# Two-chunk k/v loads, small vectors loaded contiguous and transposed, swaps partly by engine copies, the first layer norm on GpSimd as multiply-add, another planned order

## The chip, the cores and the metric

The kernel runs on one core of a Trainium2 chip. The metric is the device time of one execution in microseconds (us). Most executions of one kernel agree within 1%; a run is marked slow when it lies over 1.5% above the fastest run of the same kernel, and verdicts use the other ("fast") runs.

A core has engines that each execute their own instruction list strictly in order: TensorE (PE; its weight loads are shown as PEld), VectorE (DVE), ScalarE (ACT), GpSimd (POOL) and SyncE (SP, which here only issues DMAs). An instruction waits for semaphores that other engines or DMAs raise.

## The reference

S = 2048 positions, D = 640 channels, F = 1728, all bf16. Cut to what matters:

```python
def mix(q, k, v, shift_k, ssm_k, ssm_D):          # q is already normalized
    k_shift = sum(shift_k[:, 3 - t] * k_pad[:, t:t + S, :] for t in range(4))   # 4-tap causal filter
    kv = k_shift * v
    y = irfft(rfft(kv, 2 * S) * rfft(ssm_k, 2 * S))[:S]     # long convolution per channel
    return q * (y + kv * ssm_D)

h  = x + mix(layernorm(x), k, v, shift_k, ssm_k, ssm_D)     # x is A_q
hn = layernorm(h)
r  = hn @ w_r;  idx = top-2 positions of r                  # 2 of the 2048 positions
y  = (silu(hn[idx] @ w_gate) * (hn[idx] @ w_up)) @ w_down * sigmoid(r[idx])
out = h + hn, with y added at the two positions idx
```

## The kernel before

The 640 channels are worked on in five chunks of 128 ("chunk 0" to "chunk 4"). The convolution of a chunk is a Fourier transform written as matmuls:

1. **S1**: first stage, once for the filter and once for kv.
2. **S2**: second stage, with the constant matrix F. F is loaded compact (F2c) and expanded into four masked copies at the start ("F expansion").
3. The two **swaps** of the chunk: the spectrum of the filter lies with real parts in partitions 0 to 63 and imaginary parts in 64 to 127; a copy with the halves exchanged goes to KfB. Then the products **P1** (A times A) and **P2** (A times KfB).
4. **I1**, **I2**: the inverse, as matmuls; then I2m (times the normalized q) and I2a (the residual add).
5. A transpose and the "gram" matmuls that yield sums for the second layer norm. After the last chunk follows a serial tail: norm statistics, top-2, the small feed-forward and the output.

Every operation is declared with the engines that may run it. A list of numbers, PLAN, holds one number for each operation: bits for its place in a single global order, for its engine and for its PSUM region. Semaphore waits are derived from it. So PLAN decides the order on every engine, and each engine obeys it literally.

```python
# F expansion: 16 tiles of 1024, any of ScalarE, VectorE, GpSimd
for kq in range(4):
    for lp in range(4):
        ...
        flex(lambda e, ...: e.activation(o, i, ACTF.Copy, scale=m),
             lambda e, ...: e.tensor_scalar(o, i, m, None, op0=ALU.mult), ..., name="F2x", pool=True)

# the swap: two DMAs, in SyncE's list
for h in range(2):
    dma("sp", KfB[64*h:64*h+64, c % 2], A2[64-64*h:128-64*h, ks], ...,
        writes=[buf("KfB", c % 2, h)] + [buf("P2", c % 2, b) for b in range(2)], name="sw%d" % c)

# the products: P2 on VectorE whole, or on GpSimd in four pieces of 128x512
op("dve", lambda e: e.tensor_tensor(dst[:, :, blk], A[:, :, blk], dst[:, :, blk], ALU.mult), ...)   # P1
em["pool"] = [part(g, g + 8) for g in range(0, NG, 8)]                                             # P2

# first layer norm ("LN1"), 16 tiles; nb = -mean*rd exists already, for ScalarE's form
flex(lambda e, n2=n2: e.activation(q_sb[:, n2, :], x_sb[:, n2, :], ACTF.Identity, bias=nb[...], scale=rd[...]),
     lambda e, n2=n2: e.tensor_scalar(q_sb[:, n2, :], x_sb[:, n2, :], m32[...], rd[...],
                                      op0=ALU.subtract, op1=ALU.mult), ..., name="q", pool=True)
```

Both swap DMAs of a chunk declare that they write the same P2 buffers, so the second one waits until the first has landed.

Of the kernel before, what the change touches and what calls it, by code (L numbers as in the profile page):

```python
# [17 lines left out]
    1376, 3536, 1504, 1680, 4048, 1728, 3920, 3472, 608, 8, 1816, 2000, 408, 3344, 3408, 456, 6872, 352, 6096, 3856, 648, 2704, 2632, 160, 2760, 6145,  # L18
    6224, 2896, 2312, 7234, 6936, 7304, 7000, 7064, 2184, 96, 7107, 2952, 3032, 2264, 2520, 736, 2392, 544, 6592, 2456, 6721, 784, 6664, 7184, 3984,
    7554, 7427, 6792, 1312, 3088, 3280, 6336, 6408, 928, 976, 288, 7632, 2584, 6465, 6536, 224, 7504, 8130, 1040, 3216, 8200, 11608, 3152, 7392, 8000,  # L20
    8072, 1632, 11843, 11672, 2840, 2072, 16472, 7745, 7816, 11920, 1440, 3664, 3792, 7874, 7944, 8512, 8584, 3600, 848, 3728, 8643, 8897, 8968, 4112,
    6304, 10832, 9154, 4304, 4240, 16536, 16600, 16664, 2136, 11736, 1880, 4176, 8768, 8840, 1120, 10881, 9232, 8712, 10960, 9024, 9096, 8258, 8387,
    8456, 8336, 12000, 12064, 11800, 12320, 11329, 11400, 4624, 11456, 11528, 12128, 4368, 4432, 4496, 4560, 4688, 4744, 12192, 12256, 12419, 12496,
    12546, 1944, 12384, 11073, 11144, 21336, 11200, 12624, 11272, 4816, 4880, 5400, 5592, 5336, 16707, 21400, 16784, 12866, 12936, 21464, 21528,
    12737, 12816, 11040, 15696, 12995, 9312, 13120, 13200, 7712, 5953, 6032, 15746, 15824, 13064, 14019, 14088, 13632, 13704, 13249, 13328, 13890,
    13960, 14147, 14216, 16192, 9376, 9552, 9624, 5080, 13505, 13584, 17120, 13378, 13448, 16928, 5208, 5712, 13763, 9424, 9488, 13832, 16264, 5912,
    15937, 5528, 16066, 16136, 17056, 17184, 16008, 16864, 16992, 17283, 17360, 17408, 26072, 17488, 1184, 9794, 17248, 16323, 16400, 9921, 9864,
    14304, 5016, 26136, 17600, 17986, 17859, 9992, 21569, 17680, 18056, 5840, 17928, 15904, 17728, 17800, 1248, 10050, 14368, 21648, 21792, 9667,
    9736, 10128, 21920, 18497, 18240, 18312, 18754, 5272, 20560, 18627, 18696, 18576, 5784, 19009, 19080, 18368, 18440, 21728, 18883, 18832, 14544,
    14480, 18114, 18184, 20609, 20688, 10176, 18952, 10434, 10504, 20801, 14616, 5464, 20931, 20872, 21000, 5656, 10256, 21984, 14416, 21856, 22048,  # L30
    22144, 21186, 21256, 12704, 22224, 5144, 22273, 22352, 14787, 14856, 14912, 14984, 4952, 10320, 10384, 22658, 22728, 21057, 21136, 22787, 22856,
    19168, 22112, 26304, 26384, 22530, 22600, 19232, 22401, 22480, 10576, 20768, 25360, 14659, 14728, 15040, 10640, 15112, 23682, 22913, 22992, 23752,
    23299, 23368, 26464, 25408, 25488, 23042, 23112, 23553, 23632, 23811, 23880, 19280, 23424, 23496, 15170, 15248, 23169, 23240, 25667, 25736, 15360,
    25921, 25794, 25864, 15440, 25539, 26656, 26200, 25992, 19344, 26264, 19480, 26592, 26528, 26784, 26720, 26816, 17568, 26896, 26946, 27024, 19416,
    19521, 25608, 19592, 19648, 19720, 23968, 24032, 15504, 27459, 27536, 27330, 27400, 27201, 27072, 27280, 30176, 30240, 27144, 19907, 19976, 19778,
    28097, 28168, 24144, 19856, 28352, 28424, 24280, 28483, 28560, 27585, 27656, 27970, 28048, 27712, 27784, 27843, 27920, 28225, 1568, 28296, 28640,
    15312, 10690, 24080, 24208, 10760, 20032, 20112, 20227, 15553, 20304, 20368, 20176, 28704, 28752, 28944, 28880, 28816, 15624, 30658, 24576, 24449,
    24648, 24520, 24323, 24704, 20417, 24776, 24392, 30720, 20488, 25024, 25104, 24835, 24912, 29377, 29448, 24976, 25168, 28992, 29064, 29249, 29123,
    29328, 25216, 25296, 29192, 29505, 29584, 30784, 29699, 29648, 29888, 30848, 29776, 29960, 29840, 30017, 30096, 30912, 31056, 31120, 30976, 31184,
    31376, 31248, 31440, 31312, 31504, 31632, 30304, 31568, 31888, 31688, 31760, 31952, 32016, 32080, 31816, 32144, 32195, 30368, 30432, 34128, 30496,  # L40
    30560, 30600, 34192, 35016, 34760, 34896, 32272, 32336, 32400, 35080, 34248, 34312, 34448, 34712, 34576, 32848, 32912, 34648, 34848, 32464, 32768,
    32528, 34960, 35408, 35288, 35224, 34392, 32961, 33104, 33024, 33232, 33168, 33474, 33608, 32592, 32656, 33539, 35168, 35344, 33296, 33680, 32720,
    33744, 33352, 35488, 33424, 33793, 33936, 33872, 33984, 34064, 34528, 35544,
# [18 lines left out]
class Planned:  # L62
# [16 lines left out]
    def decl(self, emit, reads, writes, dur, dma=None, name="", region=False, uses=None):  # L79
# [5 lines left out]
        t.dma = dma  # L85
        t.reads = list(reads)
# [41 lines left out]
    def plan(self):  # L128
# [3 lines left out]
        for tid in self.order:  # L132
# [7 lines left out]
            deps = {}  # L140

# [18 lines left out]
            if t.dma is not None:  # L160
                key = self._sem("D_%d" % self.ndma)
                self.ndma += 1
                inc = 16
            else:
                key = own
                inc = 1
# [81 lines left out]
S = 2048  # L248
# [34 lines left out]
YBUF = (0,)  # L283


def build(nc, A_q, A_k, A_v, A_shift_k, A_ssm_k, A_ssm_D, B_x, B_w_r, B_w_gate, B_w_up, B_w_down, out):
# [8 lines left out]
    with es:  # L295
# [17 lines left out]
        def dma(engs, o, i, occ, reads=(), writes=(), slow=False, name=""):  # L313
            kw = dict(allow_slow_non_contiguous=True) if slow else {}
            engs = engs.split("/")
            return tr.decl({g: (lambda e: e.dma_start(o, i, **kw)) for g in engs}, reads, writes,
                           {g: 1.2 if g == "pool" else 0.45 for g in engs}, dma=occ, name="D" + name)
# [46 lines left out]
        sizes = [("k_T", kT_n), ("v_T", 2 * kT_n), ("filt_C", S), ("k_C", NP), ("P0", NP), ("P1", NP),  # L364
# [4 lines left out]
        tot = sum(n for _, n in sizes)  # L369
# [9 lines left out]
        v_T = EV["v_T"].rearrange("p (s n d) -> p s n d", s=2, n=NB)  # L379
# [11 lines left out]
        Bp = sb("Bp", [128, 2 * NB, CW], BF)  # L391
        y0 = sb("y0", [128, NB, CW], BF) if YBUF else None
# [4 lines left out]
        w_C = sb("w_C", [128, NCH, 4], BF)  # L397
        w_S = sb("w_S", [128, 2 * NCH, 2], BF)
        w_R = sb("w_R", [128, 2 * NCH, 4], BF)
        D_C = sb("D_C", [128, NCH], BF)  # L400
        wr_C = sb("wr_C", [128, NCH, 2], BF)
        wr_L = sb("wr_L", [128, NCH], BF)
# [12 lines left out]
        sprod = sb("sprod", [128, 2, 2, NB], F32)  # L415
# [4 lines left out]
        rows = sb("rows", [2, D], BF)  # L420
# [24 lines left out]

        def ld_k(c):
            for i, (a, b) in enumerate(((0, 8), (8, 16)) if c == 0 else ((0, 16),)):
                dma("sp/act" if c == 0 else "sp", k_T[:, a:b], k3[:, a:b, CW * c:CW * c + CW], 2.3 * (b - a) / 16,
                    writes=[buf("kT", i)] if c == 0 else [buf("kT", 0), buf("kT", 1)], name="kT%d%d" % (c, i))

        def ld_v(c):
            for i, (a, b) in enumerate(((0, 8), (8, 16)) if c == 0 else ((0, 16),)):
                dma("sp/act" if c == 0 else "sp", v_T[:, c % 2, a:b], v3[:, a:b, CW * c:CW * c + CW], 2.3 * (b - a) / 16,
                    writes=[buf("vT", c % 2, i)] if c == 0 else [buf("vT", c % 2, 0), buf("vT", c % 2, 1)], name="vT%d%d" % (c, i))
# [5 lines left out]
        dma("sp/act/pool", D_C[:], A_ssm_D.rearrange("(c p) -> p c", p=128), 0.4, writes=[buf("DC")], slow=True, name="DC")  # L460
        dma("sp/act/pool", w_C[:], A_shift_k.rearrange("(c p) j -> p c j", p=128), 0.4, writes=[buf("wC")], slow=True, name="wC")
# [4 lines left out]
        if STACKED:  # L466
            wsrc = A_shift_k.rearrange("(b p) j -> p b j", p=64)
            for half in range(2):
                dma("sp/act/pool", w_R[64 * half:64 * half + 64], wsrc, 0.4, writes=[buf("wR", half)], slow=True, name="wR")
                for h in range(2):  # L470
                    tp = half if h == 0 else 1 - half
                    pr_ = slice(64 * half, 64 * half + 64)
                    op("dve", lambda e, h=h, tp=tp, pr_=pr_: e.tensor_copy(w_S[pr_].rearrange("p (c h) a -> p c h a", h=2)[:, :, h, :],
                                                                            w_R[pr_].rearrange("p (c h) (a t) -> p c h a t", h=2, t=2)[:, :, h, :, tp]),
                       reads=[buf("wR", half)], writes=[buf("wS", h, half)], dur=0.17, name="wS")
# [270 lines left out]
        def frontk(c):  # L746
            b_diag(c)
            b_KT(c)
            if c + 1 < NCH:
                ld_k(c + 1)  # L750
# [308 lines left out]
```

## Time and profile before

| | before |
|---|---|
| time, median of 3 runs | 183.54 us (182.47 to 184.32) |
| span of the profiled run | 183.2 us (a run of 185.07 us, marked slow) |
| mean granted TensorE clock in it | 0.859 |
| DMA packets, of them under 512 bytes | 32125, 24862 |
| end of the S2 evacuations of chunks 0 to 4 | 47.6, 63.6, 84.8, 117.8, 132.6 us |

The profiled run is within 1% of the median, so its stage times may be used. The last table row is read from the timelines of ScalarE and VectorE: it is where the last copy "A<-ps" of each chunk ends. It marks the progress of the kernel better than any busy share.

From the page of the kernel before: busy time of each engine with its share; the chain of work that ended last, by engine and by line; then groups (line, engine, operation, output and input, shapes, count | total us, mean ns of one | idle time ahead of them and who ended it).

```profile
PE 130.1 (71%) x3050; PEld 120.5 (66%) x3050; DVE 119.1 (65%) x184; ACT 97.5 (53%) x102; POOL 106.8 (58%) x77
...
POOL 42%; PE 26%; DMA 13%; DVE 10%; issue 4%; ACT 3%; SPq 0%; DVEq 0%; POOLq 0%
...
L736 POOL TENSOR_SCALAR q_sb<-x_sb,ln 128x640 bf16<-128x640 bf16 x14 | 35.6, 2554 | 1.5 <-DVE ln L733 1.5
...
L497 POOL TENSOR_SCALAR F<-q_sb,lm 128x1024 bf16<-128x1024 bf16 x9 | 25.8, 2875 | 1.1 <-DMA q_sb<-c_F 1.1
...
L977 POOL TENSOR_SCALAR q_sb<-x_sb,ln 128x640 bf16<-128x640 bf16 x5 | 4.8, 961 | 33.0 <-DVE ln L972 33.0
...
L640 DVE TENSOR_TENSOR A<-A 128x2048 bf16<-128x2048 bf16 x10 | 14.0, 1410 | 4.5 <-DMA KfB<-A 4.5
```

GpSimd is neither the busiest engine (TensorE is) nor even the second, but it holds 42% of the chain. That is the first thing to read: who is busy most and who is waited for are different questions. The second is the pair L736 and L977. Both are a two-step scalar operation on a 128x640 bf16 tile on GpSimd, but L736 (subtract, then multiply; LN1) takes 2554 ns and L977 (multiply, then add; the final normalization) 961 ns.

GpSimd's timeline of the kernel before (start, duration, group) shows how long LN1 occupies it, with the products of chunk 1 between its tiles:

```profile
53.01 7.47 POOL L736 TENSOR_SCALAR q_sb<-x_sb,ln 128x640 bf16<-128x640 bf16 x3 [1.46 <-DVE ln L733]
...
89.17 4.46 POOL L648 TENSOR_TENSOR KfB<-A,KfB 128x512 bf16<-128x512 bf16 x4
93.61 9.95 POOL L736 TENSOR_SCALAR q_sb<-x_sb,ln 128x640 bf16<-128x640 bf16 x4
```

LN1 ends at 103.6 us. The view of waits of the kernel before (engine and line, what ended the wait: total us, times, longest) says who paid:

```profile
DVE atmp L683 <- POOL q_sb L736: 11.9, 1, 11.9
...
PE ps L619 <- POOL F L497: 6.9, 2, 4.9
...
DVE A L640 <- DMA KfB<-A: 4.5, 1, 4.5
```

VectorE stood 11.9 us for an LN1 tile, TensorE 6.9 us for F tiles. The third line is the last swap; the chain of the kernel before, in order of time, shows that it costs more than 4.5 us:

```profile
128.83 3.77 ACT A L320 x4
132.62 6.43 DMA KfB<-A
139.13 4.19 DMA KfB<-A
143.44 0.47 DVE A L640
```

From the end of S2 at 132.6 to the first product at 143.4 the chain holds nothing but the two swap DMAs, one after the other.

### The profile page before, as it was taken

To read this page: it belongs to the slowest core of one execution; us is meant where nothing else is said; L and a number is where in the kernel's file an instruction comes from. 1 tells how busy PE (TensorE), PEld (TensorE's weight loads), DVE (VectorE), ACT (ScalarE), POOL (GpSimd) and SP (SyncE) were. 2 spreads that over 40 slices of the span, in tenths; PEclk is the share of its full clock that TensorE was granted. 3 is DMA by queue.
4 is the path that set the end of the run, shared out by engine and by line. 5 is a ranking of instruction groups with operands and counts; after the bars stand their busy time and mean duration, and the time that the engine had idled before them with its cause. 6 is when DMAs were issued, how large, how long until landed. Compare 5 with 4: busy or idle time off the path is not lost.

```text
span 183.2 us, 6744 instructions
## 1 busy us (share of the span) xinstructions
PE 130.1 (71%) x3050; PEld 120.5 (66%) x3050; DVE 119.1 (65%) x184; ACT 97.5 (53%) x102; POOL 106.8 (58%) x77
## 2 busy tenths in 40 slices
PE   0555498362999838999458089999999669926781
PEld 0544397352978737999357079999988569825770
DVE  0575739850598993799400397999993696889501
ACT  0005949760885942899417118989976524236300
POOL 3037999999059999999999999103800000009002
PEclk9999569996599996999978858999999979975555
DMA  5999991791497999389981039459494935551940
GB/s 152 305 290 245 191 319 32 173 221 71 86 224 154 213 230 309 79 179 224 168 203 45 0 72 222 85 123 277 128 315 95 314 108 167 190 182 67 405 160 1
DMA packets 32125, 32.18 MB, mean 176 GB/s; under 512 B 24862, under 2 KB 27104, under 8 KB 31328
## 3 DMA queue, kind: packets, MB, share of 16 engines
q1 hardware_dynamic: 31008, 31.05, 66.9%
q10 hardware_dynamic: 1024, 0.69, 1.6%
q8 instruction: 24, 0.39, 0.9%
q0 software_dynamic: 64, 0.00, 0.3%
q14 instruction: 5, 0.04, 0.1%
HBM read 19.61 MB, written 2.62 MB: 121 GB/s over the span
## 4 chain that ended last, share of the span: by engine, by line
POOL 42%; PE 26%; DMA 13%; DVE 10%; issue 4%; ACT 3%; SPq 0%; DVEq 0%; POOLq 0%
POOL q_sb L736 18%; POOL F L497 14%; DMA q_sb<-c_F 8%; POOL KfB L648 6%; DMA KfB<-A 6%; PE ps L619 4%; PE ps L583 4%; POOL diag L516 4%; PE ps L664 4%; PE ps L665 3%; PE ps L675 2%; PE ps L946 2%; ACT A L320 2%; PE ps L558 2%; PE ps L960 2%
## 5 line engine op out<-in xcount | busy, mean ns | idle before, releaser
L736 POOL TENSOR_SCALAR q_sb<-x_sb,ln 128x640 bf16<-128x640 bf16 x14 | 35.6, 2554 | 1.5 <-DVE ln L733 1.5
L320 ACT ACTIVATE big<-ps 128x1024 bf16<-128x1024 f32 (+1 forms) x33 | 31.9, 1027 | 4.7 <-PE ps L583 4.5
L320 ACT ACTIVATE Bp<-ps 128x1024 bf16<-128x1024 f32 x17 | 17.1, 1023 | 31.6 <-PE ps L665 30.4
L320 ACT ACTIVATE A<-ps 128x1024 bf16<-128x1024 f32 x29 | 27.7, 1028 | 10.9 <-PE ps L619 10.8
L648 POOL TENSOR_TENSOR KfB<-A,KfB 128x512 bf16<-128x512 bf16 x20 | 26.5, 1361 | 11.3 <-DMA KfB<-A 11.3
L664 PE MATMUL ps<-G,A 128*128 128x128 bf16 x160 | 24.4, 251 | 9.6 <-issue 7.8
L583 PE MATMUL ps<-F,big 128*64 128x128 bf16 x640 | 24.2, 231 | 9.3 <-DVE big L320 8.3
L619 PE MATMUL ps<-big,F 128*128 128x64 bf16 x640 | 22.2, 196 | 9.1 <-POOL F L497 6.9
L583 PEld LDWEIGHTS ps<-F,big 128*64 128x64 bf16 x640 | 20.3, 117 | 12.2 <-DVE big L320 8.9
L619 PEld LDWEIGHTS ps<-big,F 128*128 128x128 bf16 x640 | 20.7, 100 | 10.3 <-POOL F L497 7.1
L497 POOL TENSOR_SCALAR F<-q_sb,lm 128x1024 bf16<-128x1024 bf16 x9 | 25.8, 2875 | 1.1 <-DMA q_sb<-c_F 1.1
L664 PEld LDWEIGHTS ps<-G,A 128*128 128x128 bf16 x160 | 18.2, 115 | 10.6 <-issue 8.3
L665 PE MATMUL ps<-G,KfB 128*128 128x128 bf16 x160 | 24.5, 252 | 0.3 <-issue 0.3
L977 POOL TENSOR_SCALAR q_sb<-x_sb,ln 128x640 bf16<-128x640 bf16 x5 | 4.8, 961 | 33.0 <-DVE ln L972 33.0
L320 DVE CAST A<-ps 128x1024 bf16<-128x1024 f32 x11 | 13.3, 1222 | 9.0 <-PE ps L619 8.7
L665 PEld LDWEIGHTS ps<-G,KfB 128*128 128x128 bf16 x160 | 18.4, 115 | 0.5 <-issue 0.5
L568 DVE TENSOR_TENSOR big<-ps,big 128x1024 bf16<-128x1024 f32 x10 | 11.9, 1218 | 8.9 <-PE ps L564 4.1
L713 DVE BATCH_NORM_STATS2 st<-x_sb 128x6 f32<-128x320 bf16 x32 | 13.3, 477 | 6.5 <-DMA x_sb<-in_A_q_dram 6.5
L640 DVE TENSOR_TENSOR A<-A 128x2048 bf16<-128x2048 bf16 x10 | 14.0, 1410 | 4.5 <-DMA KfB<-A 4.5
L516 POOL TENSOR_SCALAR diag<-cons,w_S 128x64 bf16<-128x64 bf16 x16 | 9.6, 601 | 6.2 <-PE ps L558 5.4
L320 DVE COPY big<-ps 128x2048 bf16<-128x2048 bf16 (+1 forms) x10 | 11.7, 1167 | 1.3 <-PE ps L533 0.7
L320 DVE CAST big<-ps 128x1024 bf16<-128x1024 f32 x8 | 9.7, 1221 | 4.2 <-PE ps L583 4.2
(114 smaller groups left out, 201.4 us busy)
## 6 DMA issues: line engine op xcount, KB each, us to landing
KfB<-A SPq DMA_DIRECT2D x10, 512.0 KB, 4.6
x_sb<-in_A_q_dram SPq DMA_DIRECT2D x4, 640.0 KB, 5.6
big<-in_A_ssm_k_dram SPq DMA_DIRECT2D x5, 512.0 KB, 6.6
out_dram<-q_sb SPq DMA_DIRECT2D x4, 640.0 KB, 3.5
big<-big SPq DMA_DIRECT2D x8, 260.0 KB, 4.7
big<-in_A_k_dram SPq DMA_DIRECT2D x4, 512.0 KB, 8.1
big<-in_A_v_dram SPq DMA_DIRECT2D x4, 512.0 KB, 8.2
big<-big SPq DMA_DIRECT2D x8, 243.8 KB, 3.8
```

The costliest lines, as they stand in the source:

```text
L320: return flex(lambda e: e.activation(o, i(), ACTF.Copy), lambda e: e.tensor_copy(o, i()), reads, writes, (t_act(n), t_d2(n) if bf else t_d ...
L497: flex(lambda e, o=o, i=i, m=m: e.activation(o, i, ACTF.Copy, scale=m), lambda e, o=o, i=i, m=m: e.tensor_scalar(o, i, m, None, op0=ALU.mult),
L516: op("pool", lambda e, h=h, a=a: e.tensor_scalar(diagS[:, s, h, a, :], eye2, w_S[:, 2 * c + h, a:a + 1], None, op0=ALU.mult), reads=[bI, b ...
L568: op("dve", lambda e: e.tensor_tensor(kv[:, :, 8 * hb:8 * hb + 8, :], R32(bt).rearrange("p (n g l) -> p g n l", n=8, l=4), v_T[:, s, 8 * h ...
L583: return e.matmul(R32(bt)[64 * cc:64 * cc + 64, 128 * gl:128 * gl + 128], lhsT=lt, rhs=F1[:, cc, :], start=True, stop=True, tile_position= ...
L619: bt = op("pe", [lambda e, kl=kl: e.matmul(R32(bt)[:, 64 * kl:64 * kl + 64].rearrange("p (s g) -> p s g", s=2), lhsT=F2[:, 16 * r + kl, :] ...
L640: op("dve", lambda e: e.tensor_tensor(dst[:, :, blk], A[:, :, blk], dst[:, :, blk], ALU.mult), reads=[buf("A2", ksl(c), r) for r in rs], w ...
L648: return lambda e: e.tensor_tensor(K[:, g0:g1, blk], A[:, g0:g1, blk], K[:, g0:g1, blk], ALU.mult)
L664: ems.append(lambda e, g=g, gl=gl: e.matmul(R32(bt)[:, 128 * gl:128 * gl + 128], lhsT=dst[:, g, :], rhs=G[:, 0, :], start=True, stop=False))
L665: ems.append(lambda e, g=g, gl=gl: e.matmul(R32(bt)[:, 128 * gl:128 * gl + 128], lhsT=K[:, g, :], rhs=G[:, 1, :], start=False, stop=True))
L713: op("dve", [lambda e, n2=n2, i=i: e.bn_stats(st6[:, n2, i, :], x_sb[:, n2, 320 * i:320 * i + 320]) for i in range(2)], reads=[buf("x", n2 ...
L736: lambda e, n2=n2: e.tensor_scalar(q_sb[:, n2, :], x_sb[:, n2, :], m32[:, n2:n2 + 1], rd[:, n2:n2 + 1], op0=ALU.subtract, op1=ALU.mult),
```

## The change

The intent: relieve GpSimd (LN1 in its cheaper form, F expansion moved to VectorE), shorten the swaps, fetch k and v in longer runs (two chunks, 512 bytes, at a time), replace scattered loads of small vectors by contiguous ones with tiny transposes, and plan the whole order anew around that. The diff is cut to its core; the new PLAN, small edits of planner estimates and of the tail (a bf16 product and an early reciprocal for the selected rows, the loop order of the last feed-forward matmuls, the final normalization no longer on GpSimd) are left out. So is a new rule in the derivation of waits: an operation on GpSimd now also waits for the one before it there.

```diff
-    e.tensor_scalar(q_sb[:, n2, :], x_sb[:, n2, :], m32[...], rd[...], op0=ALU.subtract, op1=ALU.mult)
+    e.tensor_scalar(q_sb[:, n2, :], x_sb[:, n2, :], rd[...], nb[...], op0=ALU.mult, op1=ALU.add)

-        for kq in range(4):                      # F expansion, 16 tiles of 1024
+        for kq in range(2):                      # 8 tiles of 2048
-                ... dur=(t_act(1024), t_d4(1024), t_p1(1024)), name="F2x", pool=True)
+                ... dur=(2.1, 0.75), name="F2x")                 # not on GpSimd

-                dma("sp", KfB[...], A2[...], 1.35, ..., name="sw%d" % c)
+                em = {"sp": lambda e, o=o, i=i: e.dma_start(o, i)}
+                if "dve" in SWAP_ON:
+                    em["dve"], du["dve"] = cp, t_d4(4096)           # one copy of 64x4096
+                if "pool" in SWAP_ON:
+                    em["pool"] = [lambda e, ...: e.tensor_copy(o[:, a:a+8, :], i[:, a:a+8, :])
+                                  for a in range(0, NG, 8)]         # four copies of 64x1024
+                tr.decl(em, kfr, ..., name="Dsw%d" % c, dmaengs=["sp"])

+        def ld_tok(c, nm, tile, src):            # k and v: two chunks in one load
+            w = min(2, NCH - c) * CW
+            for i in range(2):
+                a, b = 8 * i, 8 * i + 8
+                dma(..., tile[:, a:b, 0:w], src[:, a:b, CW*c:CW*c + w], ...)

-        dma(..., D_C[:], A_ssm_D.rearrange("(c p) -> p c", p=128), ..., slow=True)     # and w_C, w_R, wr_L
+        dma(..., tiny[:, 0:512], A_shift_k.rearrange("(c p) j -> c (p j)", c=NCH), ...)  # and D, w_r
+        pty = op("pe", [14 tiny transposes], ...)
+        op("dve", lambda e: e.tensor_copy(wDr[:], ...), ...)

-YBUF = (0,)
+YBUF = ()
-PLAN = [1376, 3536, ...]
+PLAN = [1360, 1408, ...]
```

In the new plan, of the ten half swaps five are VectorE copies (among them both of chunk 4), three GpSimd copies (among them both of chunk 0) and two stay DMAs. Of the ten P2 products seven stand on GpSimd, five did before. F is wholly on VectorE.

## The prediction

> **What bounds the kernel now.** By the chain of waits, GpSimd holds 42% of the 183.2 us span, TensorE 26%, DMA 13%, VectorE 10%. Two groups explain it: LN1's subtract-multiply (14 tiles, 2554 ns each, 35.6 us) and the F expansion (9 tiles, 2875 ns each, 25.8 us). The timeline shows their cost:
> - the first S2 stage (chunk 0) starts at 33.4 but ends near 46.6 us, because F's last quarter leaves GpSimd at 44.6;
> - LN1 starts at 53.0 and its last tile ends at 103.5; VectorE waits 11.9 us for it, and TensorE, behind VectorE, 5.9 us;
> - P2 products sit between LN1 tiles on GpSimd, and TensorE waits for them (2.9 us at 66, 4.9 us at 89);
> - in the last chunk the two swap DMAs, queued beside weight loads, hold VectorE from 132.6 to 143.4 us.
>
> Where nothing stalls (106-132 us) TensorE is 98% busy: the next bound, then VectorE.
>
> **What changes.**
> - F goes to VectorE, 8 tiles of 2048: the trace has 480 ns for 1024; estimate 0.75 us each (the Trainium skill, "VectorE: DVE Perf Modes", tier table, gives 693 ns for a 2048-element 4x operation; this trace has none of that size). GpSimd loses 25.8 us, VectorE gains about 5.
> - LN1 as multiply-add: the final normalization has the same form and shape and takes 961 ns on GpSimd. 15 x 0.96 = 14.4 us, not 35.6.
> - Swaps: of ten halves, five become VectorE copies (estimate 1.3 us each), three GpSimd copies (estimate 4 us each), two stay DMA (4.6 us). The last chunk's two are VectorE: about 3 us replaces 10.8 us.
> - k/v: 256-byte runs become 512 mostly; the skill ("DMA: Bandwidth & Descriptors", Specifications) gives 512 B as the minimum for line rate. The page counts 24862 packets under 512 B; perhaps 16000 vanish. Worth 1-2 us at the front.
> - Small vectors: scattered loads go (one issue held SP 4.5 us), 14 tiny transposes come. 1-2 us, front only.
> - Order: LN1 statistics now precede F on VectorE. VectorE's total stays about 120 us, ScalarE grows from 97.5 to about 104, GpSimd falls from 107 to about 75.
>
> **The sum.** First S2 stage done at about 40 instead of 46.6. LN1 done near 63 instead of 103.5, so it leaves the chain; the 33 us between S2 ends 84.8 and 118 shrinks to about 17. Last chunk saves 7-8 us at its swaps. Adding up TensorE's work at full clock leaves some 90 us after 36 us; at 90% use that is 100, and the tail after the last gram (160.5 to 183.2, 22.7 us) hardly changes: 36 + 100 + 23 = 159 us.
>
> **Predicted: 159 us, 8 in 10 between 149 and 170. Faster by over 2%: 0.96; within 2%: 0.03; slower: 0.01.**
>
> **Right if** LN1 tiles on GpSimd take about 1 us and end before 70 us; GpSimd falls under 20% of the chain, TensorE and VectorE lead it; no wait over 4 us for KfB before the last P1; the tail stays 22-23 us; VectorE over 72% busy.
>
> **Wrong if** GpSimd's swap copies take much over 1 us per piece and make chunk 0's inverse wait; VectorE, now carrying F and swaps, delays TensorE and the granted clock falls; contention slows GpSimd (P2 pieces vary from 1143 to 2204 ns); v's pair loads, waiting for both halves of the tile, come late and hold up the in-order SP queue behind them.

## More of the kernel before

One line of the groups view of the kernel before is needed later, the residual add:

```profile
L688 DVE TENSOR_TENSOR x_sb<-x_sb,atmp 128x1024 bf16<-128x1024 bf16 x10 | 6.7, 686 | 0.2
```

## The result

| | before | after |
|---|---|---|
| median of 4 runs each, side by side | 183.6 us (182.47 to 184.32) | 159.6 us (159.44 to 160.17) |
| span of the profiled run | 183.2 us | 158.0 us |
| mean granted TensorE clock in it | 0.859 | 0.893 |
| end of S2 evacuations, chunks 0 to 4 | 47.6, 63.6, 84.8, 117.8, 132.6 | 37.4, 51.7, 71.1, 91.0, 113.0 |
| DMA packets, under 512 bytes | 32125, 24862 | 20689, 5741 |

The ratio is 0.8703 (95% interval 0.8653 to 0.8753): 13% faster. Such ratios are the mean time of one kernel's fast runs over that of the other's fast runs of the same rounds, so they are not quite the ratio of the medians that are quoted. Where microseconds are worked out from a ratio below, they are the ratio's distance times 184.

From the page of the kernel after, in the same order of views as before:

```profile
PE 121.6 (77%) x3063; PEld 112.0 (71%) x3063; DVE 126.2 (80%) x184; ACT 103.2 (65%) x106; POOL 83.2 (53%) x84
...
PE 27%; DVE 23%; issue 9%; ACT 8%; POOL 1%; DVEq 0%; ACTq 0%
...
L660 POOL TENSOR_TENSOR KfB<-A,KfB 128x512 bf16<-128x512 bf16 x28 | 38.6, 1407 | 2.0 <-DVE KfB L608 1.5
...
L652 DVE TENSOR_TENSOR A<-A 128x2048 bf16<-128x2048 bf16 x10 | 17.4, 1741 | 0.8 <-POOL KfB L614 0.8
L748 POOL TENSOR_SCALAR q_sb<-x_sb,ln 128x640 bf16<-128x640 bf16 x15 | 16.4, 1094 | 1.5
...
L614 POOL COPY KfB<-A 64x1024 bf16<-64x1024 bf16 x12 | 12.9, 1113 | 2.3 <-DVE KfB L608 2.1
```

GpSimd left the chain (42% to 1%); no DMA is in it. VectorE is now the busiest engine, and its products P1 (L652, the old L640) have become slower, 1741 ns instead of 1410, though nobody touched them.

The groups view of the kernel after has the smaller ones:

```profile
L700 DVE TENSOR_TENSOR x_sb<-x_sb,atmp 128x1024 bf16<-128x1024 bf16 x10 | 11.1, 1127 | 0.2
...
L608 DVE COPY KfB<-A 64x4096 bf16<-64x4096 bf16 x5 | 6.1, 1222 | 0.2
...
L500 DVE TENSOR_SCALAR F<-q_sb,lm 128x2048 bf16<-128x2048 bf16 x8 | 5.5, 749 | 0.0
```

GpSimd's timeline after has LN1 from 31.4 to 67.1 us, with chunk 0's swap copies and products between:

```profile
31.41 5.11 POOL L748 TENSOR_SCALAR q_sb<-x_sb,ln 128x640 bf16<-128x640 bf16 x5
...
40.18 8.03 POOL L614 COPY KfB<-A 64x1024 bf16<-64x1024 bf16 x8
48.30 6.45 POOL L660 TENSOR_TENSOR KfB<-A,KfB 128x512 bf16<-128x512 bf16 x4
...
64.29 2.80 POOL L748 TENSOR_SCALAR q_sb<-x_sb,ln 128x640 bf16<-128x640 bf16 x2
```

VectorE's timeline after, from two places: a product beside GpSimd's products (48.3) and one beside LN1 tiles only (64.2), then the last swap.

```profile
48.34 2.19 DVE L652 TENSOR_TENSOR A<-A 128x2048 bf16<-128x2048 bf16 x1 [0.80 <-POOL KfB L614]
...
64.15 1.22 DVE L652 TENSOR_TENSOR A<-A 128x2048 bf16<-128x2048 bf16 x1
...
113.29 2.48 DVE L608 COPY KfB<-A 64x4096 bf16<-64x4096 bf16 x2
115.80 1.22 DVE L652 TENSOR_TENSOR A<-A 128x2048 bf16<-128x2048 bf16 x1
```

From the end of S2 (113.0) to the first product behind the swap (115.8) it is 2.8 us now, and was 10.8.

The span splits into the front (to the first end of S2), the middle, and the tail after the last gram, whose first instruction is a statistic on VectorE, at 162.4 before and 139.2 after: 47.6 + 114.8 + 20.8 before, 37.4 + 101.8 + 18.8 after. So 10 us came from the front, 13 from the middle and 2 from the tail.

In the middle TensorE not only stood less, its work also took less time. The view of windows gives for a stretch its bounds and length, then the busy time (and count) of PE, PEld, DVE, ACT and POOL, then the granted clock, the DMA share and GB/s. First the middle of before (this window was cut at 160.5), then that of after:

```profile
47.60:160.50 112.90, 93.15 (x2253) 86.71 (x2249) 81.66 (x83) 70.66 (x72) 67.89 (x42) 0.92 0.70 172
37.40:139.20 101.80, 86.85 (x2309) 79.82 (x2303) 89.76 (x78) 72.12 (x72) 66.39 (x58) 0.99 0.56 154
```

TensorE's busy time fell by 6.3 us with 56 matmuls more, and the granted clock rose from 0.92 to 0.99. In before, read in windows of 4 us, low clocks come right after stretches in which TensorE mostly stood: 0.69 at 71 to 75 us, after 1.8 us of work in the 4 us before, and 0.50 at 107 to 111, after 0.8 us. After has 1.00 in every such window from 37 to 137 us, even behind the one from 53 to 57 with 1.9 us of work, so no threshold can be read from this. Of the 11.1 us between the two windows a little over half is shorter busy time of TensorE, which came along with the shorter waits. No run sets the clock apart from the waits.

### The profile page after: what moved, and what is told of

It is laid out like the page before. It is cut to its first block, busy times and chain, and to the rows that moved or that the text cites. A ratio compares the mean times of both kernels' runs of the same rounds, so it can differ in the third digit from the quotient of the medians.

```text
span 158.0 us, 6763 instructions
## 1 busy us (share of the span) xinstructions
PE 121.6 (77%) x3063; PEld 112.0 (71%) x3063; DVE 126.2 (80%) x184; ACT 103.2 (65%) x106; POOL 83.2 (53%) x84
## 2 busy tenths in 40 slices
DMA packets 20689, 27.97 MB, mean 177 GB/s; under 512 B 5741, under 2 KB 16180, under 8 KB 20404
## 4 chain that ended last, share of the span: by engine, by line
PE 27%; DVE 23%; issue 9%; ACT 8%; POOL 1%; DVEq 0%; ACTq 0%
PE ps L587 5%; DVE atmp L698 4%; DVE x_sb L700 4%; ACT A L324 3%; DVE big L324 3%; PE ps L631 3%; PE ps L562 3%; PE ps L687 3%; ACT Bp L324 3%; PE ps L962 2%; DVE big L572 2%; DVE A L652 2%; PE ps L676 2%; DVE KfB L608 2%; PE ps L677 1%
## 5 line engine op out<-in xcount | busy, mean ns | idle before, releaser
L324 ACT ACTIVATE big<-ps 128x1024 bf16<-128x1024 f32 (+2 forms) x40 | 42.0, 1092 | 19.7 <-PE ps L587 11.2
L660 POOL TENSOR_TENSOR KfB<-A,KfB 128x512 bf16<-128x512 bf16 x28 | 38.6, 1407 | 2.0 <-DVE KfB L608 1.5
L587 PEld LDWEIGHTS ps<-F,big 128*64 128x64 bf16 x640 | 20.1, 116 | 11.1 <-DVE big L572 4.8
L631 PE MATMUL ps<-big,F 128*128 128x64 bf16 x640 | 23.2, 198 | 5.9 <-ACT big L324 2.5
L324 ACT ACTIVATE Bp<-ps 128x1024 bf16<-128x1024 f32 x17 | 16.8, 1024 | 8.0 <-PE ps L677 7.9
L519 POOL TENSOR_SCALAR diag<-cons,wDr 128x64 bf16<-128x64 bf16 x16 | 10.6, 664 | 20.2 <-PE ps L568 11.8
L676 PE MATMUL ps<-G,A 128*128 128x128 bf16 x160 | 19.2, 219 | 1.4 <-ACT Bp L324 1.4
L677 PE MATMUL ps<-G,KfB 128*128 128x128 bf16 x160 | 19.1, 219 | 0.0
L652 DVE TENSOR_TENSOR A<-A 128x2048 bf16<-128x2048 bf16 x10 | 17.4, 1741 | 0.8 <-POOL KfB L614 0.8
L748 POOL TENSOR_SCALAR q_sb<-x_sb,ln 128x640 bf16<-128x640 bf16 x15 | 16.4, 1094 | 1.5
L725 DVE BATCH_NORM_STATS2 st<-x_sb 128x6 f32<-128x320 bf16 x32 | 12.9, 483 | 4.5 <-DMA x_sb<-in_A_q_dram 4.5
L698 DVE TENSOR_TENSOR atmp<-q_sb,ps 128x1024 bf16<-128x1024 bf16 x10 | 12.1, 1215 | 4.7 <-PE ps L687 4.7
L572 DVE TENSOR_TENSOR big<-ps,big 128x1024 bf16<-128x1024 f32 x10 | 12.0, 1215 | 3.6 <-PE ps L568 2.9
L324 DVE CAST A<-ps 128x1024 bf16<-128x1024 f32 x11 | 13.2, 1217 | 1.8 <-PE ps L631 1.8
L614 POOL COPY KfB<-A 64x1024 bf16<-64x1024 bf16 x12 | 12.9, 1113 | 2.3 <-DVE KfB L608 2.1
L687 PE MATMUL ps<-Bp,H 128*128 128x128 bf16 x160 | 10.5, 219 | 2.2 <-issue 1.6
```

What stands on the lines that cost most here:

```text
L324: return flex(lambda e: e.activation(o, i(), ACTF.Copy), lambda e: e.tensor_copy(o, i()), reads, writes, (t_act(n), t_d2(n) if bf else t_d ...
L572: op("dve", lambda e: e.tensor_tensor(kv[:, :, 8 * hb:8 * hb + 8, :], R32(bt).rearrange("p (n g l) -> p g n l", n=8, l=4), v_T[:, 8 * hb:8 ...
L587: return e.matmul(R32(bt)[64 * cc:64 * cc + 64, 128 * gl:128 * gl + 128], lhsT=lt, rhs=F1[:, cc, :], start=True, stop=True, tile_position= ...
L614: em["pool"] = [lambda e, o=o, i=i, a=a: e.tensor_copy(o[:, a:a + 8, :], i[:, a:a + 8, :]) for a in range(0, NG, 8)]
L631: bt = op("pe", [lambda e, kl=kl: e.matmul(R32(bt)[:, 64 * kl:64 * kl + 64].rearrange("p (s g) -> p s g", s=2), lhsT=F2[:, 16 * r + kl, :] ...
L660: return lambda e: e.tensor_tensor(K[:, g0:g1, blk], A[:, g0:g1, blk], K[:, g0:g1, blk], ALU.mult)
```

## The experiments

Twelve kernels ran, all with correct results, on three chips. Each was timed against the kernel before in the same rounds (median there: 184.9, 185.1 and 183.8 us), so kernels are compared by their ratios. The kernel after stands at 0.8703. The two questions were: which parts make the 24 us, and do the terms of the prediction hold when one is taken away alone? Two theories stood at first: (A) the prediction's, GpSimd's time on the chain is what fell, and the rest is small; (B) the new order and the swaps are what counts, and the cheaper operations alone would run into the next wait.

### e1: LN1 alone, in the old order

```diff
 # kernel before
-  ... m32[:, n2:n2 + 1], rd[:, n2:n2 + 1], op0=ALU.subtract, op1=ALU.mult)
+  ... rd[:, n2:n2 + 1], nb[:, n2:n2 + 1], op0=ALU.mult, op1=ALU.add)
```

> The kernel before, with one line changed: LN1's subtract-multiply becomes multiply-add; engines and order stay as they were. My theory (GpSimd's LN1 is the largest single cost): tiles fall from 2.55 to about 1.0 us, the TensorE gaps at 66, 89 and 100 us shrink by about 3.6, 4.9 and 6 us; 170 us, between 166 and 174. Rival (the loads and the new order made the gain, GpSimd was only late and not limiting): 180 us or more.

Measured: 172.47 us, ratio 0.9342 (0.9258 to 0.9426): 12 us from one line. From its page:

```profile
L736 POOL TENSOR_SCALAR q_sb<-x_sb,ln 128x640 bf16<-128x640 bf16 x14 | 14.0, 1007 | 1.5 <-DVE ln L733 1.5
```

GpSimd saved 21.6 us (35.6 to 14.0), the kernel 12. The view of waits tells where the difference went:

```profile
POOL KfB L648 <- DMA KfB<-A: 20.4, 4, 7.7
```

In the old order GpSimd now waits 20.4 us for swap DMAs; it waited 11.3 us before. That much of (B) is right: the saved time runs partly into the next wait.

### e2: F expansion alone on VectorE, in the old order

```diff
 # kernel before, after the plan is read
+for t in tr.tasks:
+    if t.name == "F2x":
+        t.eng = "dve"
```

> The kernel before, with only the F expansion moved to VectorE (all 16 tiles of 1024), same order otherwise. My theory: the first S2 stage ends near 39 instead of 46.6 us and LN1 starts some 7 us sooner; 177 us, between 174 and 180. Rival (VectorE is too full at the front, so the wait only changes its name): 182 us or more.

Measured: 178.2 us, ratio 0.9683 (0.9603 to 0.9763), 6 us. The first S2 ends at 40.7 instead of 47.6, and LN1 starts at 46.0 instead of 53.0. The front is worth about what the first S2 gains.

### e3: LN1, F and the last swap together, in the old order

```diff
 # kernel before; LN1 as in e1, F as in e2, and
+    if t.name == "Dsw4":                  # both halves, declared with a VectorE copy as well
+        t.eng, t.dma = "dve", None
```

> The kernel before with three edits and the old order and old loads: LN1 as multiply-add, F on VectorE, and the last chunk's two swap halves as VectorE copies. My theory (these three carry the gain): about 160 us, between 156 and 165. Rival (the new order, the two-chunk loads and the contiguous small vectors carry a third of the gain or more): 168 us or more.

Measured: 165.86 us, ratio 0.8979 (0.8904 to 0.9054): 19 us of the 24, between the two expectations. Three local edits make four fifths of the gain; the order, the loads, the small vectors, the other swaps and the edits of the tail make the rest, about 5 us (0.898 against 0.870). The three are worth 18.8 us together, and e1 and e2 already 12.1 and 5.8 apart, so the last swap adds only about 1 us here if the gains of e1 and e2 simply add up (LN1 and F together, without the swap, were not run), not the 7 to 8 that the prediction gave it. The profiles fit that. In before VectorE stood 4.5 us for these DMAs, and the two copies that replace them take 2.5 of its own time. In e3 the first product behind the swap still starts 9.1 us after the end of S2 (126.9 against 117.8), where before has 10.8: the old order keeps VectorE's other work between the two copies. The profile of e3 (taken in a slow run, so only used for what waits for what) has GpSimd waiting 22.8 us for the other swap DMAs.

### e4: the kernel after with the old LN1

```diff
 # kernel after
-  ... rd[:, n2:n2 + 1], nb[:, n2:n2 + 1], op0=ALU.mult, op1=ALU.add)
+  ... m32[:, n2:n2 + 1], rd[:, n2:n2 + 1], op0=ALU.subtract, op1=ALU.mult)
```

> The kernel after with LN1 put back to subtract-multiply, nothing else. My theory: 15 tiles at 1.5 us more delay the first products on GpSimd by about 12 us and those of the next chunk by about 20; 178 us, between 172 and 184. Rival (in the new order LN1 has slack): under 166 us.

Measured: 181.74 us, ratio 0.9898 (0.980 to 0.9996). The one line is worth 12 us in the old order and 22 us in the new one (0.9898 against 0.8703). From the page of e4, the chain and LN1:

```profile
POOL 42%; PE 30%; DVE 12%; ACT 5%; issue 5%; DMA 4%; ACTq 1%; POOLq 0%; DVEq 0%
...
L748 POOL TENSOR_SCALAR q_sb<-x_sb,ln 128x640 bf16<-128x640 bf16 x15 | 39.0, 2599 | 1.5
```

GpSimd is back at 42% of the chain. The new plan lets the swap copies of chunk 0 follow eight LN1 tiles on GpSimd, so slow tiles now hold up a swap as well: in e4 these copies start at 52.9 instead of 40.2, 12.7 us later, and the eight tiles took 12.9 us longer (21.0 against 8.1). Theory (A) holds for the mechanism; of (B) it holds that a part's worth depends on the order around it.

### e5: the kernel after with all ten half swaps as DMAs

```diff
 # kernel after, after the plan is read
+    if t.name.startswith("Dsw"):
+        t.eng = "sp"
```

> The kernel after with all ten swap halves as DMAs again, same order otherwise. VectorE loses 5 x 1.22 us of copies and GpSimd 12.9 us, but each swap then waits some 5 us for its DMA, and the last chunk's has nothing to hide behind. My theory (only the last chunk's copies matter; the others are hidden and cost VectorE work): 162 us, between 159 and 166, and no more than the run with only the last swap as a DMA. Rival (copies help in every chunk): over 167 us.

Measured: 196.95 us, ratio 1.0698 (1.0600 to 1.0796), slower than the kernel before. The expectation was wrong by 35 us. Waits of e5:

```profile
DVE A L652 <- DMA KfB<-A: 28.8, 3, 22.4
POOL KfB L660 <- DMA KfB<-A: 28.5, 4, 12.4
...
PE ps L562 <- DMA big<-big: 12.2, 1, 12.2
```

VectorE and GpSimd each wait about 28 us for swaps. The third line is another victim: "big<-big" are the DMAs that stack shifted copies of k, which stand in SyncE's list too. The list of SyncE obeys the order of the plan, and an issue that waits for its data holds up all issues behind it. The plan had placed these swaps for engines, not for that list. The Trainium skill ("DMA: Bandwidth & Descriptors", "Anatomy of one DMA", implications) says that the DMA engines do not wait on semaphores and that the wait takes place on the issuing sequencer before dispatch; the trace agrees with it here.

### e6: only the last chunk's two half swaps as DMAs

```diff
 # kernel after, after the plan is read
+    if t.name == "Dsw4":
+        t.eng = "sp"
```

> The kernel after with only the last chunk's two swap halves as DMAs. My theory: the last products start 4 to 7 us later, because the DMA lands 5 us or more after its issue and queues with the weight loads: 165 us, between 162 and 168. Rival (the last inverse of the chunk before fills the wait): under 161 us.

Measured: 176.13 us, ratio 0.9489 (0.9373 to 0.9604): 14 us lost by the ratios, against an expected 5. SyncE's timeline of e6:

```profile
111.30 7.27 SPq L320 DMA_DIRECT2D big<-in_B_w_up_dram  x2
124.24 0.37 SPq L320 DMA_DIRECT2D big<-in_B_w_down_dram  x1
125.20 6.74 SPq L609 DMA_DIRECT2D KfB<-A  x2
```

The data of the swap are ready at about 113.6 us, but feed-forward weight loads stand in front of it in the list and wait for each other; the swap is issued 11.6 us late. Its two halves then land one after the other, at 131.5 and 135.6. The waits of e6:

```profile
DVE A L652 <- DMA KfB<-A: 21.8, 1, 21.8
```

### e11: the same, with the weight loads moved behind the swaps

```diff
 # e6, and
+late = [i for i in tr.order if tr.tasks[i].name in ("Dwg", "Dwu", "Dwd")]
+tr.order = [i for i in tr.order if i not in late]
+k = max(j for j, i in enumerate(tr.order) if tr.tasks[i].name == "Dsw4") + 1
+tr.order[k:k] = late
```

> The kernel after with the last chunk's two swap halves as DMAs, but the weight loads moved behind them in SP's order. My theory: most of the 16 us that the DMA form cost stood in SP's in-order queue (issued at 125.2 us although the data was there at 113); issued at once, the swap lands 5 us later and costs 2 to 4 us: 162.5 us, between 160.5 and 166. Rival (the transfer itself is slow beside other traffic): 170 us or more.

Measured: 171.37 us, ratio 0.933 (0.9273 to 0.9387), which is inside what the rival expected. But the trace does not show the rival's reason alone. SyncE's timeline of e11:

```profile
113.62 4.64 SPq L609 DMA_DIRECT2D KfB<-A  x2
118.42 9.12 SPq L320 DMA_DIRECT2D big<-in_B_w_gate_dram  x2
131.65 6.43 SPq L320 DMA_DIRECT2D big<-in_B_w_up_dram  x2
142.39 13.69 SPq L320 DMA_DIRECT2D big<-in_B_w_down_dram  x4
156.18 3.20 SPq L320 DMA_DIRECT2D out_dram<-q_sb  x4
```

The swap is issued at once now, and takes 4.16 and 4.20 us by the chain of e11. The product behind it starts at 122.1 instead of 115.8: the direct cost of the DMAs is 6.3 us. But the weight loads hold the list for 38 us (118.4 to 156.1), and the output stores stand behind them; the first store is issued at 156.2, where the kernel after has it at 144.5, and an output store of 7.8 us ends the chain. So the weights' delay was not taken away, only moved to the end. The run shows the direct cost; it does not give a clean price of the list position, since both orders pay it somewhere. To price it alone another list than SyncE's would have to carry the weights; that was not run. Nor was a swap whose two DMAs are under way together: the second half waits for the first only because both declare the same P2 buffers, so part of the 6.3 us may belong to that declaration.

### e7: the kernel after with all P2 products on VectorE

The kernel after had slower products on VectorE. The theory here was contention: P1 runs slower while GpSimd runs P2. The rival was that P1 is slow by its place, or by the clock.

```diff
 # kernel after, after the plan is read
+    if t.name.startswith("P2"):
+        t.eng = "dve"
```

> The kernel after with all P2 products on VectorE. They add 7 x 1.22 = 8.5 us to it, but take GpSimd's two-input products away, beside which VectorE's own two-SBUF-input products are slow (P1 1741 ns on the mean against 1215 undisturbed, the residual add 1127 against 680: about 10 us in all). My theory (contention is what VectorE pays for GpSimd's help): 159 us, between 156 and 162, P1 under 1.3 us and the add under 0.75 us. Rival (VectorE is full and 8.5 us more of it cost time): 164 us or more.

Measured: 172.9 us, ratio 0.9339 (0.9239 to 0.944), 12 us slower than the kernel after. P1 takes 1217 ns, as expected. The residual add takes 856, where under 750 was expected: eight of the ten adds take 0.69 us, but the two that run beside GpSimd's swap copies take 1.52 each. So the theory of contention holds, and for GpSimd's copies as well as for its products. The time was missed, for one wait. The waits of e7:

```profile
DVE KfB L660 <- POOL KfB L614: 12.2, 1, 12.2
```

The plan has the first P2 product of chunk 0 early, where GpSimd would have waited for its own swap copies anyway. On VectorE the same place in the order makes VectorE stand 12.2 us for them, with all its later work behind.

### e10: e7 with that one product moved to its neighbour

```diff
 # e7, and
+p2 = {t.name: t.tid for t in tr.tasks if t.name in ("P200", "P201")}
+tr.order.remove(p2["P200"])
+tr.order.insert(tr.order.index(p2["P201"]), p2["P200"])
```

> The kernel after with all P2 on VectorE, as before, but chunk 0's first P2 moved down VectorE's order to stand beside its second, after GpSimd's swap copy is done. My theory: the run without this move lost 12.2 us in one in-order wait of VectorE for that copy, and nothing to the 8.5 us of added work, which the vanished contention pays for; so about 161 us, between 157 and 164. Rival (VectorE has no room for the products): 168 us or more.

Measured: 160.99 us, ratio 0.8786 (0.8728 to 0.8845; two of the four runs count as slow). Moving one instruction in the order brought back 10 us (0.9339 to 0.8786). From the page of e10:

```profile
PE 122.5 (78%) x3063; PEld 113.2 (72%) x3063; DVE 126.2 (81%) x191; ACT 103.0 (66%) x106; POOL 48.0 (31%) x56
...
L652 DVE TENSOR_TENSOR A<-A 128x2048 bf16<-128x2048 bf16 x10 | 12.7, 1266 | 0.9 <-POOL KfB L614 0.9
```

VectorE does all ten P2 products in the same 126.2 us in which the kernel after did three. So seven P2 products on GpSimd, 38.6 us of its time for all 28 pieces, relieved VectorE by nothing: what they took off came back as slower P1 products and residual adds. The intervals of e10 and of the kernel after overlap, so neither is better.

### e9: P2 on VectorE, the swaps of chunks 0 to 3 as DMAs

```diff
 # e7, and
+    if t.name in ("Dsw0", "Dsw1", "Dsw2", "Dsw3"):
+        t.eng = "sp"
```

> As the run before it (all P2 on VectorE), and the swaps of the first four chunks by DMA; the last chunk's stay VectorE copies. GpSimd keeps only LN1 and the diagonals. VectorE loses 3 x 1.22 us and all contention. My theory: 156 us, between 153 and 160. Rival (swap latency matters in each chunk): 162 us or more.

Measured: 186.03 us, ratio 1.006 (0.9963 to 1.0156). The hope was to empty GpSimd and keep only the short swap where it matters. In this order the wait for a swap matters in every chunk; waits of e9:

```profile
DVE KfB L660 <- DMA KfB<-A: 20.6, 3, 8.8
```

TensorE again waits 12.2 us for the stacking DMAs, as in e5; the victim of the swaps is VectorE's P2 now. This run had e7's badly placed product in it as well, so it says nothing about DMA swaps in an order planned for them.

### e8a and e8b: the run length of the k and v loads

In e8a each two-chunk load is cut into two DMAs of one chunk each (256-byte runs); in e8b, the control, into two DMAs of half the rows (512-byte runs). Both have the same bytes, count of DMAs and places in the order. (For both, the completion semaphore counts 16 for each of the DMAs.)

```diff
 # kernel after; e8a
+pcs = [(tile[:, a:b, CW*j:CW*j+CW], src[:, a:b, CW*(c+j):CW*(c+j)+CW]) for j in range(w // CW)]
 # e8b
+pcs = [(tile[:, m:m+4, 0:w], src[:, m:m+4, CW*c:CW*c+w]) for m in (a, a + 4)] if w > CW else ...
 # both: one task that issues every piece of pcs
```

> The kernel after with each two-chunk k/v load issued as two DMAs of one chunk's columns each: 256-byte runs again, the same bytes at the same place in the order, one more issue each. If the run length matters, the front's k and v land later and the first products of chunk 0 with them: 161.5 us, between 160.5 and 163.5, with the first SC product on VectorE 1 to 2 us later than 23.3. If only issues count, the same as the control with two row halves.

> The control: each two-chunk k/v load issued as two DMAs of half the rows each: 512-byte runs, as many DMAs as the run before. 159.8 us, between 159.2 and 160.6: one more issue each costs under half a per cent.

Measured: e8a 160.72 us (157.94 to 162.45), e8b 156.87 (155.76 to 158.78), ratio of e8b 0.8524 (0.8468 to 0.858). Packets under 512 bytes are 22253 in e8a and 5869 in e8b, a difference of 16384. The medians are 3.9 us apart; but four of the six runs of e8a count as slow, and the two fast runs average 158.0 against 156.7 for e8b's five, 1.3 us. So the worth of the longer runs is 1 to 4 us, of the expected sign and not settled closer; e8b itself came out 3 us below what was expected. VectorE's timeline shows where it enters. In e8a the first F tile waits for its load (the number in brackets):

```profile
28.74 0.75 DVE L503 TENSOR_SCALAR F<-q_sb,lm 128x2048 bf16<-128x2048 bf16 x1 [2.15 <-DMA q_sb<-c_F]
```

In e8b it does not:

```profile
26.35 0.74 DVE L503 TENSOR_SCALAR F<-q_sb,lm 128x2048 bf16<-128x2048 bf16 x1
```

It is not k or v that come late (the first product with v starts at 23.4 in e8a and 23.2 in e8b, where a delay of 1 to 2 us was expected), but the second load of F. It is issued at 22.5 in e8a and at 18.2 in e8b, mostly because the issues of the four v loads before it in SyncE's list take 6.8 us against 3.2. From issue to landing the loads of F take about the same in both (6.3 and 6.1 us, median of two). The first S2 ends at 40.2 against 37.3. The Trainium skill ("DMA: Bandwidth & Descriptors", Specifications) names 512 bytes as the least transfer for line rate; both runs agree in direction, with 2.4 us between the first F tiles.

e8b also came out ahead of the kernel after (0.8524 against 0.8703). They did not run side by side, so whether cutting loads by rows is a gain of 2% or a difference between chips stays open. It is the lowest time seen, and not claimed as a better version.

## Why the prediction was right, point by point

The time was predicted as 159 us, and is 159.6. The mechanism holds; that the number agrees so closely is partly luck. The sum was 36 + 100 + 23; on the trace it is 37.4 + 101.8 + 18.8 = 158.0, so two terms were 3.2 us too low together and one 4.2 too high. And the sum was one of spans, which lie 1.8 us below the times (183.2 against 185.07, 158.0 against 159.76); the prediction left that out.

- **LN1 leaves the chain.** Right, and shown from both sides (e1: 12 us, e4: 22 us). It ends at 67.1 us instead of the predicted 63. A tile takes 1094 ns instead of 961, so 16.4 us instead of 14.4: most take 0.87 us, but three that start just after a two-input product or a swap copy on VectorE take 1.73 to 1.90.
- **F on VectorE.** 0.75 us a tile was predicted, 0.749 measured; 6 us for the kernel (e2). The Trainium skill's "VectorE: DVE Perf Modes", tier table, gave 693 ns for such a tile, and the run decides for 749.
- **Front: 37.4 measured.** The prediction has two figures for it, "about 40" in words and 36 in the sum. The eight F tiles run on VectorE from 26.4 to 31.9 us; in before the last left GpSimd at 44.6.
- **Middle: 100 predicted, 101.8 measured.** The prediction took 90 us of TensorE work at 90% use; it was 86.9 us of busy time at 85%. "At full clock" came true: the granted clock was 0.99 there, and 0.92 in before. The 33 us between the S2 ends of chunks 2 and 3 became 19.9, predicted 17.
- **Tail: "hardly changes" from 22.7; measured 18.8.** This term was mis-sized by its boundary: at 160.5 the last gram of before had not ended. From the same instruction on, before takes 20.8 us. The real gain is 2.0 us; no run separates the tail edits.
- **VectorE's total of "about 120" failed; it is 126.2.** What was missing is the slowing by GpSimd: P1 17.4 us instead of 14.0 and the residual add 11.1 instead of 6.7, 7.8 us together. e10 shows the cause: with no products on GpSimd, P1 takes 1266 ns and the add 855. The rest of the add's excess is two adds that run beside GpSimd's swap copies and take 1.52 us each; the other eight take 0.69. The Trainium skill ("SBUF — State Buffer", practical consequences of the port table) says that a VectorE instruction with two inputs in SBUF (the memory of the kernel's tiles; PSUM takes the results of the matmuls) contends with a GpSimd instruction that reads SBUF, and one with at most one SBUF input outside the two-port modes does not. The trace agrees on both: 2.19 us beside GpSimd's products against 1.22 alone, while the product of v with a PSUM tile stays at 1215 ns, 1218 before. Which of the two pays differs: P1 at 64.15 us took its 1.22 although an LN1 tile ran beside it, and that tile, which started after it, took 1.83 us instead of 0.87; at 48.3 the piece on GpSimd had started first, and P1 took 2.19. The prediction had listed contention as a risk to GpSimd; the engine that suffered on the chain was VectorE.
- **GpSimd's total of "about 75" failed; it is 83.2.** The plan moved two more P2 products there, eight pieces of 1.4 us, 11 us; the sum left them out.
- **Swaps.** The piece costs were right (VectorE copy 1.3 predicted, 1.222 measured; GpSimd 4 a half predicted, 8.03 for two measured), and from S2's end to the product the last chunk saves 8.0 us (10.8 to 2.8), 7 to 8 predicted. The step that failed is "hold VectorE from 132.6 to 143.4 us": the trace has VectorE at other work until 138.9, so most of that stretch was not lost. What the last swap is worth for the total is another number: about 1 us on top of LN1 and F in the old order (e3, by subtraction), 14 us in the new (e6). At the product behind the swap the DMAs themselves cost 6.3 us (e11); the rest is put down to the in-order list of SyncE, where the trace of e6 shows an issue 11.6 us late, but no run prices it alone.
- **Small packets.** 16000 were predicted to vanish; 19121 did, 16384 by the run length (e8a against e8b), so about 2700 are left for the small vectors, by subtraction. The time was put at 1 to 2 us; 1 to 4 was measured. The small vectors were not tested alone.
- **What was named as the sign of being right** came out: GpSimd below 20% of the chain (1%), TensorE and VectorE leading (27% and 23%), no wait over 4 us for KfB before the last P1 (0.8 us in all), VectorE over 72% busy (80%). Only the tail of 22 to 23 us did not.

What stays open: how the 5 us beyond e3 split into order, loads, small vectors, the other swaps and the tail, apart from the 1 to 4 us of the run length; and how much of the middle's gain the higher clock would give by itself.

## What to carry to other kernels

Look for the engine that is waited for, not the one that is busiest, and compare its instructions with others of the same shape: the same normalization cost 2554 ns on GpSimd as subtract-multiply and 961 as multiply-add, and one line was worth 12 to 22 us. Where engines and a DMA list execute in order, an operation's engine and its place in the order are one decision: four of these runs (e5, e6, e7, e9) moved work to another engine without planning its place and lost 12 to 37 us against the kernel after, and moving a single instruction won 10 of them back. Before giving an engine's two-input work to a neighbour, check that the first engine gets faster in total: here VectorE's busy time was 126.2 us with seven of the ten P2 products on GpSimd, and 126.2 with none there.

## What the Trainium skill lacked or had wrong

- **GPSIMD Engine Reference** (4.1 Engine selection, and 3.1): it calls one-input work roughly line rate and gives a best case of about 1.8 cycles per element at 1.2 GHz. Multiply-add on 128x640 is near that (861 to 1050 ns, worked out as 1.6 to 2.0 cycles); subtract-multiply of the same shape took 2554 ns, 4.8 cycles. No page has that the pair of operations matters by a factor of 2.7.
- **The same page**: a single multiply that expands F took 2875 ns for 1024 elements, 3.4 cycles each. No page explains it; why it is slow was not tested. VectorE did twice the elements in 749 ns.
- **SBUF — State Buffer** (practical consequences): the rule of contention held, but the page has no measured size for VectorE's two-input operations. Here P1 went from 1.22 us to as much as 2.23 beside GpSimd's two-input products, and the residual add from 0.69 to 1.5 to 1.7 beside products or copies there (686 ns to 1127 on average).
- **VectorE: DVE Perf Modes** (tier table): 693 ns for a 2048-element bf16 scalar operation; 749 ns here, 8% more, for a tile with a scattered output. For two SBUF tensors it has 1224 ns, and P1 undisturbed took 1217.
